# Zeros on TensorE before the queries come, split first loads, half-width value loads and other DMA costs in an order planner

## The chip, the cores and the metric

The kernel runs on one core of one Trainium2 chip, as one launch. The metric is the device time of that launch in microseconds (us), as a median over executions. TensorE (PE) multiplies; VectorE (DVE), ScalarE (ACT) and GpSimd (POOL) work on elements; SyncE (SP) issues nearly all DMAs of this kernel, in order, on one queue.

## What is computed

Three blocks follow one another: attention with a threshold (scores more than tau under their row's maximum get no weight), a token and channel mixer, and a gated two-layer block with a convolution of three taps along the sequence. Four batches (B = 4), 8 heads of 64, 576 rows, 512 channels.

```python
def _attn_ref(q, k, v, tau):                       # q, k, v: (4, 8, 576, 64)
    scores = scale * np.matmul(q, k.transpose(0, 1, 3, 2))
    thresh = np.max(scores, axis=-1, keepdims=True) - tau
    scores = np.where(scores >= thresh, scores, -1000000000.0)
    scores = scores - np.max(scores, axis=-1, keepdims=True)
    attn = np.exp(scores)
    attn = attn / (np.sum(attn, axis=-1, keepdims=True) + 1e-09)
    return np.matmul(attn, v)
...
    h = np.maximum(xt @ w_tok1, 0.0) @ w_tok2      # mixer: over the rows, then over the channels
    u = x + h.transpose(0, 2, 1)
    h2 = np.maximum(u @ w_ch1, 0.0) @ w_ch2
    x = u + h2
...
    h = np.maximum(x @ w_in, 0.0)                  # gated block; conv_w has three taps
    for k in range(K):
        conv_out += conv_w[k][None, None, :] * hp[:, k:k + S, :]
    gate = 1.0 / (1.0 + np.exp(-conv_out))
    return h * gate @ w_out
```

## The kernel before, in words

**Attention.** Per batch there are four pairs of heads, and per pair nine chunks of 128 query rows (`NSL`; the fifth chunk holds the last 64 rows of both heads), so 36 chunks per batch (`PER`). A chunk runs through: `scores` (PE, fp32 in batch 0, L527), the row maximum `nm` (DVE, L548), a threshold (L558), the exponential `e` (ACT, L560), the mask (DVE, L567), an fp16 high part `ph` (ACT, L572) and its low part (POOL, L576), a DMA transpose of both (SP, L581, the tile `pt`), and the product with v (PE, `pv`, L591 and L594). In batch 0 the tiles `e`, `ph` and `pt` of a chunk are pieces of `act_t`, four of each, in turn; later they come from a ring of 15 buffers. `norm`, `tok` and `dense` follow: the token mixer per pair of heads, the channel mixer (L758, L776) and the gated block (L809, L832) per batch. While `dense(b)` runs, `attention(b + 1)` is woven into it. Batch 0's attention has only the conversion of weights beside it.

**Loads.** `prep` loads a pair. q comes in one DMA of 128x576 fp32 (L447) and is scaled by ACT in one instruction (L461); each head's k comes in one of 64x576 (L452). v comes with its rows laid out twice, as nine slots of 64 columns: five slots hold the first layout (rows 0 to 575, 128 at a time), the other four hold the same rows shifted by half a slot. One DMA per head loads all nine (L483, 288 KB). POOL scales them (L492), ACT makes the fp16 high part `vh` of all nine (L493, or L488 for the second head in batch 0), POOL or DVE the low part `vl` of five (L494, L489). Weights come as 64-bit floats in two 32-bit halves (`wload`, L325) and are put together by ACT, DVE and POOL (L362 to L366, L350 to L352). The three taps of the convolution, `conv_w`, are loaded ahead of everything but tau.

**Order.** The instructions are built first; `Order` then puts them on their engines' queues by a list schedule. `cost` has the planned duration of an engine's instruction; `send` has for a DMA the planned time that it takes up the DMA queue, the time to issue it, and its latency; in `run` the DMA queue is one server (`queued`), and a transpose holds SP until the queue is free. Of the instructions that are ready, the one that stands first in the program goes first. The engines then keep that order whatever the chip's times are.

Of the kernel before, what the change touches and what calls it, by code (L numbers as in the profile page):

```python
# [20 lines left out]
class Order:  # L21
# [109 lines left out]
    def send(self, x):  # L131

        i = self.ins[x]
        if i.opcode == "DmaTransposeAnt":
            return 1000, 1300, 1950, 1400
        o, s = self.area(i.outs[0]), self.area(i.ins[0])
        size = o[7] * o[8] * o[6]
        return size / 330 + (50 if size < 1e5 else 0), 500, 1450, 1250 if s[9] and o[9] else 1750 if o[9] else 1300
# [4 lines left out]
    def run(self):  # L143
# [10 lines left out]
        rows, tiled, lands = {}, False, []  # L154
# [20 lines left out]
        for _ in range(n):  # L175
# [4 lines left out]
            if self.dma[x]:  # L180
# [4 lines left out]
                if self.ins[x].opcode == "DmaTransposeAnt":  # L185
                    free[e] = max(free[e], queued)
                if e == "SP":
                    queued = max(queued, t + 700) + work
                    done = max(free[e] + least, queued + land)
                else:  # L190
                    done = max(free[e] + least, t + 700 + work + land)
# [41 lines left out]
def kernel(ctx: ExitStack, tc: tile.TileContext, q, k, v, tau,  # L233
# [7 lines left out]
    nc = tc.nc  # L241
# [38 lines left out]


# [37 lines left out]
    ps = psum.tile([P, 8, 512], F32, name="ps")  # L319
# [85 lines left out]
    if conv_w.dtype == F32:  # L405
        nc.sync.dma_start(cw, conv_w)
    else:
        float32(cw, cw, *load_hl(conv_w, 0, 3 * NG), 0)
# [17 lines left out]
    for vh, _ in v_t:  # L426
        V.memset(vh[:, :, :, D:D + 1], ONE)
    act_t = const.tile([P, NF * 2, S], F16, name="act_t")
# [12 lines left out]
    def prep(b, p):  # L441
# [4 lines left out]
        if b < NB32:  # L446
            nc.sync.dma_start(f32(qt), q[b, p])  # L447
            for h in range(2):
                if b == 0:
# [11 lines left out]
            A.activation(out=t, in_=t, func=AF.Copy, scale=qsc[:, 0:1])  # L461
# [19 lines left out]
        for hh in range(2):  # L481
            t = qk2.tile([P, S], F32, tag="x", name="ld", bufs=15)
            nc.sync.dma_start(t, v[b, 2 * p + hh])  # L483
            vn.append(t.rearrange("p (a d) -> p a d", d=D))
        yield
        for hh in range(2):
            if b == 0 and hh:
                A.activation(out=vh[:, hh, :, 0:D], in_=vn[hh], func=AF.Copy, scale=VSC)  # L488
                V.scalar_tensor_tensor(out=vl[:, hh], in0=vn[hh][:, 0:NS + 1], scalar=VSC, in1=vh[:, hh, 0:NS + 1, 0:D],  # L489
                                       op0=ALU.mult, op1=ALU.subtract)  # L490
            else:
                G.tensor_scalar(out=vn[hh], in0=vn[hh], scalar1=VSC, scalar2=1.0, op0=ALU.mult, op1=ALU.mult)  # L492
                A.activation(out=vh[:, hh, :, 0:D], in_=vn[hh], func=AF.Copy)  # L493
                G.tensor_tensor(out=vl[:, hh], in0=vn[hh][:, 0:NS + 1], in1=vh[:, hh, 0:NS + 1, 0:D], op=ALU.subtract)  # L494
# [370 lines left out]
    for n, _ in enumerate(attention(0)):  # L865
        if n == NW:
# [75 lines left out]
```

## Time and profile before

| | |
|---|---|
| median of 3 executions | 775.82 us |
| lowest and highest | 774.68 and 777.67 us |
| profiled execution | 773.05 us, of which 771.2 us is the span from the first to the last instruction |
| mean granted TensorE clock in the span | 0.993 of full |
| PE busy | 721.5 us, 94% |
| DVE, ACT, POOL busy | 506.5, 459.0, 425.9 us |

The page of the profile has the busy times, a strip of 40 slices of 19.3 us each with the busy tenths of every engine, the granted clock of PE, the DMA load, and the costliest groups of instructions by line. Further views used here: a table of windows (busy time of each engine in a stretch), the timeline (instructions in order of time, neighbours of a kind merged, with the idle time ahead of them and what ended it), the waits (who waited for whom), the groups of instructions by line and shape, and the DMA issues of a stretch with their time from issue to landing.

### The profile page before, as it was taken

Reading aid. Unit: us, or ns where it says so; the run is one execution under the profiler, and the core shown is the slowest. Engines: PE = TensorE matmul, PEld = TensorE weight load, DVE = VectorE, ACT = ScalarE, POOL = GpSimd, SP = SyncE. Lnnn points to the kernel's source line nnn. Section 1 sums busy time; section 2 is a strip of 40 time slices with the busy share of each in tenths; the row PEclk is TensorE's granted clock in tenths of the full one; section 3 lists DMA queues with packets and bytes.
Section 4 is the critical chain, followed back from the end, with each engine's and each line's share of the span. In section 5 each row is a group of like instructions: output and inputs, shape, how many; then the busy total and the mean of one; then the engine's idle time right before and its main releaser. Section 6 shows DMA issues by size and latency. Waiting matters only on the chain. (4 is left out here: it accounts for less than half of the span.)

```text
span 771.2 us, 18502 instructions
## 1 busy us (share of the span) xinstructions
PE 721.5 (94%) x7388; PEld 541.5 (70%) x7388; DVE 506.5 (66%) x913; ACT 459.0 (60%) x926; POOL 425.9 (55%) x463
## 2 busy tenths in 40 slices
PE   5779969999998789999999999999999999999998
PEld 3457757777776646788888766778888766878764
DVE  5968977887779971676867962676876951323470
ACT  6967857786758852576557753675656841211371
POOL 5967778887877990367464850367564830000040
PEclk9999989999999999999999999999999999999999
DMA  9999988999898602568876402577853400000001
GB/s 288 210 217 187 200 193 208 230 230 229 199 238 199 147 27 93 111 153 169 155 142 144 80 23 88 131 136 158 155 123 64 79 29 35 1 1 2 1 1 62
DMA packets 196199, 99.02 MB, mean 128 GB/s; under 512 B 174224, under 2 KB 177808, under 8 KB 196112
## 3 DMA queue, kind: packets, MB, share of 16 engines
q1 hardware_dynamic: 195792, 97.57, 58.2%
q8 instruction: 58, 0.95, 0.5%
q10 hardware_dynamic: 320, 0.26, 0.1%
q14 instruction: 29, 0.24, 0.1%
HBM read 43.54 MB, written 4.72 MB: 63 GB/s over the span
## 5 line engine op out<-in xcount | busy, mean ns | idle before, releaser
L576 POOL TENSOR_TENSOR ph<-e,ph 128x576 f16<-128x576 f32 x108 | 142.5, 1319 | 110.4 <-ACT ph L572 99.3
L776 PE MATMUL ps<-act_t,wc_h 128*128 128x256 f16 (+1 forms) x768 | 149.8, 286 | 0.0
L567 DVE SCALAR_TENSOR_TENSOR e<-ps,thr,e 128x576 f32<-128x576 f32 x108 | 87.9, 814 | 53.6 <-ACT e L560 40.8
L548 DVE TENSOR_REDUCE nm<-ps 128x1 f32<-128x576 f32 x144 | 108.0, 750 | 19.6 <-PE ps L536 10.5
L799 POOL TENSOR_TENSOR act_t<-ct,act_t 128x576 f16<-128x576 f32 x32 | 47.2, 1474 | 128.4 <-ACT act_t L798 127.0
L758 PE MATMUL ps<-u_h,wc_h 128*128 128x320 f16 (+1 forms) x384 | 109.4, 286 | 0.3 <-DVE act_t L733 0.3
L776 PE MATMUL ps<-act_t,wc_l 128*128 128x256 f16 (+1 forms) x384 | 109.7, 286 | 0.0
L758 PE MATMUL ps<-u_h,wc_l 128*128 128x320 f16 (+1 forms) x384 | 109.5, 286 | 0.0
L758 PE MATMUL ps<-u_l,wc_h 128*128 128x320 f16 (+1 forms) x384 | 109.1, 286 | 0.0
L758 PEld LDWEIGHTS <-wc_h 128*128 128x128 f16 x768 | 75.1, 98 | 21.5 <-issue 2.1
L776 PEld LDWEIGHTS <-wc_h 128*128 128x128 f16 x768 | 75.1, 98 | 21.0 <-issue 1.6
L809 PE MATMUL ps<-u_h,wi_h 128*128 128x256 f16 (+1 forms) x256 | 73.2, 286 | 7.1 <-ACT h L785 4.5
L832 PE MATMUL ps<-wo_h,act_t 128*128 128x512 f16 x256 | 76.2, 379 | 0.9 <-POOL act_t L799 0.9
L794 DVE SCALAR_TENSOR_TENSOR ct<-h,cw,ct 128x576 f32<-128x576 f32 x64 | 70.6, 1106 | 8.2 <-ACT ct L792 7.7
L572 ACT ACTIVATE ph<-e 128x576 f16<-128x576 f32 x108 | 73.1, 677 | 1.0 <-DVE e L567 0.8
L733 DVE SCALAR_TENSOR_TENSOR act_t<-ps,act_t 128x256 f16<-128x256 f32 x96 | 43.6, 456 | 45.2 <-ACT act_t L732 44.8
L809 PE MATMUL ps<-u_h,wi_l 128*128 128x256 f16 (+1 forms) x256 | 73.1, 286 | 0.0
L809 PE MATMUL ps<-u_l,wi_h 128*128 128x256 f16 (+1 forms) x256 | 73.1, 286 | 0.0
L591 PE MATMUL ps<-vh,pt 128*128 128x65 f16 (+1 forms) x1080 | 68.3, 194 | 1.0 <-DVE x L614 0.8
L732 ACT ACTIVATE act_t<-ps 128x256 f16<-128x256 f32 x96 | 39.0, 408 | 46.1 <-PE ps L758 45.4
L832 PEld LDWEIGHTS <-act_t 128*128 128x128 f16 x384 | 36.5, 98 | 42.7 <-POOL act_t L799 1.5
L591 PEld LDWEIGHTS <-pt 128*128 128x128 f16 (+1 forms) x1080 | 60.8, 101 | 8.0 <-issue 4.7
(120 smaller groups left out, 1675.0 us busy)
## 6 DMA issues: line engine op xcount, KB each, us to landing
st<-in_moe_w_ch_dram SPq DMA_DIRECT2D x24, 512.0 KB, 4.8
ld<-in_v_dram SPq DMA_DIRECT2D x32, 288.0 KB, 4.1
kt<-ks SPq DMA_DIRECT2D x32, 144.0 KB, 2.8
st<-in_moe_w_in_dram SPq DMA_DIRECT2D x8, 512.0 KB, 4.7
st<-in_moe_w_out_dram SPq DMA_DIRECT2D x8, 512.0 KB, 4.2
out_dram<-ot SPq DMA_DIRECT2D x16, 256.0 KB, 2.0
qt<-in_q_dram SPq DMA_DIRECT2D x8, 288.0 KB, 5.2
kt<-in_k_dram SPq DMA_DIRECT2D x16, 144.0 KB, 4.2
```

The source lines that it names most:

```text
L548: V.tensor_reduce(out=nm, in_=c["s3"], axis=AX.XY, op=ALU.max, negate=True)
L567: V.scalar_tensor_tensor(out=e3, in0=c["s3"], scalar=c["thr"], in1=e3, op0=ALU.is_ge, op1=ALU.mult)
L572: A.activation(out=c["ph"][:, 0:S], in_=c["e"], func=AF.Copy)
L576: G.tensor_tensor(out=c["ph"][:, S:], in0=c["e"], in1=c["ph"][:, 0:S], op=ALU.subtract)
L591: T.matmul(dst[o:o + m], pt[:, j, o:o + m], vh[:, hh, j, 0:D + 1], start=(j == 0), stop=(j == NSL - 1))
L733: V.scalar_tensor_tensor(out=r_t(f, 1)[:, sl], in0=t, scalar=0.0, in1=r_t(f, 0)[:, sl], op0=ALU.max, op1=ALU.subtract)
L758: T.matmul(t, wc1[wx][:, f, c], u[c][ux][:, sl], start=(c == 0 and i == 0), stop=(c == NC - 1 and i == 2))
L776: T.matmul(t, wc2[wx][:, c, f], r_t(f, rx)[:, sl], start=(by_dve(c) and f == 0 and i == 0), stop=(f == NF - 1 and i == 2))
L794: V.scalar_tensor_tensor(out=ct, in0=ht[:, kk:kk + S], scalar=cw[:, kk, f:f + 1], in1=ct, op0=ALU.mult, op1=ALU.add)
L799: G.tensor_tensor(out=g_t(f, 1), in0=ct, in1=g_t(f, 0), op=ALU.subtract)
L809: T.matmul(t, wi[wx][:, f, c], u[c][ux][:, s0:s0 + n], start=(c == 0 and i == 0), stop=(c == NC - 1 and i == 2))
L832: T.matmul(t, g_t(f, gx)[:, j * P:(j + 1) * P], wo[wx][:, f], **lim)
```

## The change

1. PE gets ten matmuls of 128x512 zeros (fp16, from `act_t`, into the PSUM bank that `pv` uses later) as its first work; DVE writes the zeros first of all.
2. The first pair's q is loaded and scaled in two parts, 128 columns and 448 columns, with the first head's k between them.
3. The load of the taps and their conversion moves from the front to step 57 of batch 0's attention (`load_taps`).
4. v is loaded with five slots in place of nine (160 KB in place of 288 KB per head), and POOL and ACT work on five. The other four slots of `vh` are copied inside SBUF by two DMAs per pair, one per half of the partitions, after the high parts are made. Column 65 of `vh` is written too, since the copies read whole rows.
5. The planner's DMA costs change: a transpose takes up the queue for 1100 ns (1000 before), a large copy is planned at 390 bytes per ns and a small one at 300 (330 and 50 ns more for small ones before), and the first copy behind a transpose costs 550 ns more from HBM, 150 ns more from SBUF. All queues are put in order by the new sums.

```diff
         if i.opcode == "DmaTransposeAnt":
-            return 1000, 1300, 1950, 1400
+            return 1100, 1300, 1950, 1400
...
-        return size / 330 + (50 if size < 1e5 else 0), 500, 1450, ...
+        return size / (390 if size > 2e5 else 300), 500, 1450, ...
...
                     free[e] = max(free[e], queued)
+                    turns = True
+                elif turns:
+                    turns, work = False, work + (150 if self.area(self.ins[x].ins[0])[9] else 550)
...
+    V.memset(act_t[:, 0, 0:512], 0.0)
+    for _ in range(10):
+        T.matmul(ps[:, 7], act_t[:, 0, 0:P], act_t[:, 0, 0:512], start=True, stop=True)
...
-            nc.sync.dma_start(f32(qt), q[b, p])
+            first = [slice(0, P), slice(P, S)] if (b, p) == (0, 0) else [slice(0, S)]
+            nc.sync.dma_start(f32(qt)[:, first[0]], q[b, p, :, first[0]])
             for h in range(2):
+                if h and len(first) > 1:
+                    nc.sync.dma_start(f32(qt)[:, first[1]], q[b, p, :, first[1]])
...
-            A.activation(out=t, in_=t, func=AF.Copy, scale=qsc[:, 0:1])
+            for sl in first:
+                A.activation(out=t[:, sl], in_=t[:, sl], func=AF.Copy, scale=qsc[:, 0:1])
...
-            t = qk2.tile([P, S], F32, tag="x", name="ld", bufs=15)
-            nc.sync.dma_start(t, v[b, 2 * p + hh])
+            t = qk2.tile([P, S], F32, tag="x", name="ld", bufs=15)[:, 0:(NS + 1) * D]
+            nc.sync.dma_start(t, v[b, 2 * p + hh, :, 0:(NS + 1) * D])
...
-                A.activation(out=vh[:, hh, :, 0:D], in_=vn[hh], func=AF.Copy)
-                G.tensor_tensor(out=vl[:, hh], in0=vn[hh][:, 0:NS + 1], in1=vh[:, hh, 0:NS + 1, 0:D], op=ALU.subtract)
+                A.activation(out=vh[:, hh, 0:NS + 1, 0:D], in_=vn[hh], func=AF.Copy)
+                G.tensor_tensor(out=vl[:, hh], in0=vn[hh], in1=vh[:, hh, 0:NS + 1, 0:D], op=ALU.subtract)
+            if hh:
+                nc.sync.dma_start(vh[0:D, :, NS + 1:], vh[D:P, :, 0:NS])
+                nc.sync.dma_start(vh[D:P, :, NS + 1:], vh[0:D, :, 1:NS + 1])
...
+        if n == NW // 2:
+            load_taps()
```

Three places show what the new order does on SP's queue. In its rows `st` is a staging tile for weights or taps, `qt` and `kt` are a pair's q and k, `ld` is v as loaded, `vh` its high part, and `act_t<-act_t` is the transpose of a chunk of batch 0. At the start of the program, before:

```order
L296 DMA tau_t<-in_tau_dram 128x1
L325 DMA st<-in_moe_conv_w_dram 128x48
L447 DMA qt_157<-in_q_dram 128x576
L452 DMA kt_0_158<-in_k_dram 64x576
L452 DMA kt_1_159<-in_k_dram 64x576
L483 DMA ld<-in_v_dram 128x576 x2
```

The same place now:

```order
L305 DMA tau_t<-in_tau_dram 128x1
L459 DMA qt_163<-in_q_dram 128x128
L466 DMA kt_0_164<-in_k_dram 64x576
L462 DMA qt_163<-in_q_dram 128x448
L466 DMA kt_1_165<-in_k_dram 64x576
L498 DMA ld<-in_v_dram 128x320 x2
```

The taps are gone from here, a short q comes first, and the rest of q stands behind the first k. From the first weights to the fifth transpose, still on SP, before:

```order
L325 DMA st<-in_moe_w_tok_dram 128x1024 x2
L325 DMA st<-in_moe_w_tok_dram 128x512
L483 DMA ld<-in_v_dram 128x576 x6
L581 DMA_TRANSPOSE act_t<-act_t 128x9x128 x3
L325 DMA st<-in_moe_w_tok_dram 128x576
L581 DMA_TRANSPOSE act_t<-act_t 128x9x128
```

The same place now:

```order
L333 DMA st<-in_moe_w_tok_dram 128x1024 x2
L511 DMA vh_159<-vh_159 64x2x264
L333 DMA st<-in_moe_w_tok_dram 128x512
L498 DMA ld<-in_v_dram 128x320 x5
L599 DMA_TRANSPOSE act_t<-act_t 128x9x128
L512 DMA vh_159<-vh_159 64x2x264
L599 DMA_TRANSPOSE act_t<-act_t 128x9x128 x2
L333 DMA st<-in_moe_w_tok_dram 128x576
L599 DMA_TRANSPOSE act_t<-act_t 128x9x128
```

Five shorter v loads stand where six stood, and the two copies of `vh` came between. In the middle of batch 0's attention, on SP, before:

```order
L325 DMA st<-in_moe_w_ch_dram 128x1024 x2
L581 DMA_TRANSPOSE act_t<-act_t 128x9x128 x3
L325 DMA st<-in_moe_w_ch_dram 128x1024
L447 DMA qt_160<-in_q_dram 128x576
L452 DMA kt_1_162<-in_k_dram 64x576
L581 DMA_TRANSPOSE act_t<-act_t 128x9x128 x6
```

The same place now:

```order
L333 DMA st<-in_moe_w_ch_dram 128x1024 x2
L498 DMA ld<-in_v_dram 128x320
L599 DMA_TRANSPOSE act_t<-act_t 128x9x128 x2
L511 DMA vh_159<-vh_159 64x2x264
L599 DMA_TRANSPOSE act_t<-act_t 128x9x128 x2
L512 DMA vh_159<-vh_159 64x2x264
L599 DMA_TRANSPOSE act_t<-act_t 128x9x128 x2
L459 DMA qt_166<-in_q_dram 128x576
L466 DMA kt_1_168<-in_k_dram 64x576
```

The transposes now stand in shorter groups, with copies of `vh` and one v load between them. From the first to the 36th transpose of batch 0 SP issues 23 other DMAs before and 35 now: nine copies of `vh`, the taps, one v load and one k load more.

## Rows read from the trace of the kernel before

**Rows 1.** The page: span, busy times, and PE's strip of 40 slices.
```profile
span 771.2 us, 18502 instructions
PE 721.5 (94%) x7388; PEld 541.5 (70%) x7388; DVE 506.5 (66%) x913; ACT 459.0 (60%) x926; POOL 425.9 (55%) x463
...
PE   5779969999998789999999999999999999999998
```
**Rows 2.** Windows: stretch, its length, busy us of each engine, clock, DMA share, GB/s.
```profile
0.00:10.00 10.00, 3.68 (x8) 2.71 (x9) 2.98 (x21) 4.04 (x8) 4.37 (x12) 1.00 0.74 201
10.00:20.00 10.00, 6.33 (x26) 3.39 (x24) 8.54 (x17) 9.28 (x16) 6.39 (x6) 1.00 1.07 364
...
120.00:160.00 40.00, 39.66 (x391) 29.73 (x390) 33.64 (x68) 31.18 (x63) 35.59 (x41) 1.00 0.91 224
```
**Rows 3.** Windows again: batch 0's attention, its end, and the weave with batch 1.
```profile
15.00:41.00 26.00, 18.46 (x178) 11.85 (x175) 23.24 (x50) 23.88 (x48) 24.61 (x28) 0.93 1.04 237
41.00:101.00 60.00, 49.90 (x669) 38.24 (x670) 49.75 (x113) 45.69 (x81) 44.35 (x45) 1.00 1.11 201
101.00:114.00 13.00, 8.64 (x91) 6.62 (x92) 7.87 (x17) 6.60 (x12) 9.88 (x12) 0.74 0.87 200
225.00:285.00 60.00, 48.51 (x554) 35.33 (x552) 58.38 (x89) 47.15 (x93) 54.40 (x48) 1.00 0.63 144
```
**Rows 4.** Timeline of the first 24 us: start, length, engine, line, what [idle before, releaser].
```profile
6.32 5.23 PE L527 MATMUL ps<-kt,qt 128*128 128x288 f32 x12 [6.32 <-ACT qt L461]
...
8.62 0.76 DVE L548 TENSOR_REDUCE nm<-ps 128x1 f32<-128x576 f32 x1 [4.25 <-PE ps L527]
...
10.54 0.76 DVE L548 TENSOR_REDUCE nm<-ps 128x1 f32<-128x576 f32 x1 [0.91 <-PE ps L527]
...
12.40 0.81 DVE L567 SCALAR_TENSOR_TENSOR act_t<-ps,thr,act_t 128x576 f32<-128x576 f32 x1
```
**Rows 5.** Groups by line and shape, at 6 to 10.4 us and at 38 to 44 us.
```profile
L527 PE MATMUL ps<-kt,qt 128*128 128x288 f32 x9 | 4.5, 685 | 6.3 <-ACT qt L461 6.3
...
L527 PE MATMUL ps<-kt,qt 128*128 128x288 f32 x12 | 3.6, 428 | 0.0
```
**Rows 6.** DMA issues of short stretches at the start: xcount, KB, us to landing.
```profile
st<-in_moe_conv_w_dram SPq DMA_DIRECT2D x1, 24.0 KB, 2.4
...
qt<-in_q_dram SPq DMA_DIRECT2D x1, 288.0 KB, 3.7
...
kt<-in_k_dram SPq DMA_DIRECT2D x1, 144.0 KB, 3.6
...
act_t<-act_t SPq DMA_TRANSPOSE x1, 5.7
```
**Rows 7.** Timeline of SP's issues.
```profile
1.18 0.42 SPq L325 DMA_DIRECT2D st<-in_moe_conv_w_dram  x1
1.64 0.43 SPq L447 DMA_DIRECT2D qt<-in_q_dram  x1
...
15.32 6.08 SPq L581 DMA_TRANSPOSE act_t<-act_t  x3
...
63.92 1.13 SPq L454 DMA_DIRECT2D kt<-in_q_dram  x2
...
221.56 2.45 SPq L472 DMA_DIRECT2D qt<-qs  x4
```
**Rows 8.** Waits between 15 and 101 us: who waited for whom, us, times, longest.
```profile
PE ps L591 <- DMA act_t<-act_t: 8.5, 7, 2.9
...
ACT act_t L572 <- DMA act_t<-act_t: 6.8, 7, 2.7
PE ps L527 <- DVE act_t L567: 6.8, 6, 2.7
```
**Rows 9.** Groups by line and shape: ACT and POOL at two widths.
```profile
L493 ACT ACTIVATE vh<-ld 128x576 f16<-128x576 f32 x28 | 18.9, 676 | 10.8 <-POOL ld L492 10.8
...
L653 ACT ACTIVATE u_h<-ps 128x320 f16<-128x320 f32 x16 | 6.9, 428 | 3.4 <-PE ps L646 3.2
```

More of the change, by code (lines that the diff above doesn't have):

```diff
@@ L134, in send @@
         if i.opcode == "DmaTransposeAnt":
-            return 1000, 1300, 1950, 1400
+            return 1100, 1300, 1950, 1400
         o, s = self.area(i.outs[0]), self.area(i.ins[0])
         size = o[7] * o[8] * o[6]
-        return size / 330 + (50 if size < 1e5 else 0), 500, 1450, 1250 if s[9] and o[9] else 1750 if o[9] else 1300
+        return size / (390 if size > 2e5 else 300), 500, 1450, 1250 if s[9] and o[9] else 1750 if o[9] else 1300
     LAP = {"DVE": 85, "Activation": 103, "Pool": 44}
@@ L153, in run @@
         end = start = queued = 0.0
-        rows, tiled, lands = {}, False, []
+        rows, tiled, lands, turns = {}, False, [], False
         def offer(x):
@@ L279 @@
     V, A, G, T = nc.vector, nc.scalar, nc.gpsimd, nc.tensor
+    ps = psum.tile([P, 8, 512], F32, name="ps")
+    act_t = const.tile([P, NF * 2, S], F16, name="act_t")
+    V.memset(act_t[:, 0, 0:512], 0.0)
+    for _ in range(10):
+        T.matmul(ps[:, 7], act_t[:, 0, 0:P], act_t[:, 0, 0:512], start=True, stop=True)
     one = const.tile([P, 1], F32, name="one")
@@ L317 @@
     wo = wpair([P, NG, C], "wo")
-    ps = psum.tile([P, 8, 512], F32, name="ps")
     CB = 4
@@ L404, with load_taps @@
     cw = const.tile([P, 3 * NG], F32, name="cw")
[L405 to L408, printed above, removed]
+    taps = cw
+    def load_taps():
+        if conv_w.dtype == F32:
+            nc.sync.dma_start(taps, conv_w)
+        else:
+            float32(taps, taps, *load_hl(conv_w, 0, 3 * NG), 0)
     cw = cw.rearrange("p (k g) -> p k g", k=3)
@@ L426 @@
     for vh, _ in v_t:
-        V.memset(vh[:, :, :, D:D + 1], ONE)
-    act_t = const.tile([P, NF * 2, S], F16, name="act_t")
+        V.memset(vh[:, :, :, D:D + 2], ONE)
     NSL = 2 * NS + 1
@@ L487, in prep @@
             if b == 0 and hh:
-                A.activation(out=vh[:, hh, :, 0:D], in_=vn[hh], func=AF.Copy, scale=VSC)
-                V.scalar_tensor_tensor(out=vl[:, hh], in0=vn[hh][:, 0:NS + 1], scalar=VSC, in1=vh[:, hh, 0:NS + 1, 0:D],
+                A.activation(out=vh[:, hh, 0:NS + 1, 0:D], in_=vn[hh], func=AF.Copy, scale=VSC)
+                V.scalar_tensor_tensor(out=vl[:, hh], in0=vn[hh], scalar=VSC, in1=vh[:, hh, 0:NS + 1, 0:D],
                                        op0=ALU.mult, op1=ALU.subtract)
```

## The prediction

> **What bounds the kernel now.** The page comes first: PE is busy for 721.5 of 771.2 us, and its strip is at 9 from the seventh slice on, with 5 to 9 ahead of that [rows 1]. So PE sets the time for most of the run, and what can be gained is its idle time, 50 us, most of which lies in batch 0's attention. The windows say where: in the first 10 us PE is busy for 3.68 us, in the next ten for 6.33, while from 120 to 160 us it is busy for 39.66 of 40 [rows 2]. From 15 to 101 us it is idle for 26.0 - 18.46 + 60.0 - 49.90 = 17.6 us, and from 225 to 285 us for 11.5 us, where DVE works 58.38 of 60 us [rows 3].
>
> What bounds the start is a chain: q lands, ACT scales it, PE begins at 6.32 us, DVE takes the first maximum at 8.62 and the second at 10.54, the first mask follows at 12.40 [rows 4]. From then on DVE, ACT and POOL are each busy for 89 to 95% of 15 to 41 us [rows 3]. After 41 us none of them is over 83%, and the DMA share is 1.11: here the loop of the transposes counts. A chunk's high part is written over the tile that the transpose four chunks earlier reads, so ACT waits for landings (6.8 us, 7 times), and PE waits for them itself (8.5 us, 7 times); PE's waits for the mask, which frees the PSUM banks, are 6.8 us [rows 8].
>
> **The sum** is made against the profiled execution, 773.05 us: the span of 771.2 and 1.85 around it. The median of the runs is 775.82, 2.8 us more; I take the difference that the sum gives from the median.
>
> **The start (parts 1, 2, 3).** Without the taps the first q load goes out at 1.18 in place of 1.64 us, and the first k at 1.64 [rows 7]. 24 KB landed 2.4 us after issue, 288 KB after 3.7, a k behind 312 KB after 3.6 [rows 6]. The 64 KB of q so land at 3.6 to 4.9, nearer the small load, say 3.9, and k at 4.0 to 5.2, say 4.6. ACT scales 128 columns in under the 0.43 us that 320 take [rows 9]. So data would let PE begin at about 4.6. The zeros stand ahead of it: 10 matmuls of 512 columns are 5120 columns, 2.1 us at 2.4 GHz and 4.3 us at 1.2 GHz (an estimate from the two levels of the clock), from about 1.1 us, when DVE has written them: they end at 3.2 to 5.4. I take the late end, 5.4, 0.9 us ahead of 6.32.
>
> Which level is it? The windows print a clock of 1.00 for the first 10 us, but the same matmul takes 685 ns there and 428 ns at 38 to 44 us [rows 5]: PE began at its lower level. Nine records take 4.5 us there, 0.50 each, and twelve take 3.6 later, 0.30 each. A chunk is four records: 2.0 us cold, 1.2 us warm. If the zeros raise the clock in time, the first maximum can start at 5.4 + 1.2 + 0.3 (the lag in 6.32 + 2.0 to 8.62) = 6.9, 1.7 us earlier; if not, 7.7, 0.9 us earlier. The second chunk needs the rest of q: 432 KB are loaded by then, about what lay up to the first k before (456 KB, landed at 2.1 + 3.6 = 5.7), so 5.3, and 0.6 us of ACT (between the 428 and 676 ns of [rows 9]): 5.9. PE is free at 6.6, ends the chunk at 7.8, and the second maximum comes at 8.1 in place of 10.54, 2.4 us earlier. Since DVE has few gaps from the second maximum on, that is the shift I carry. Its ends: -0.9 (a cold start and no more), and -3.9, which is what the lighter loads would give. Up to the first transpose ten v loads of 288 KB become nine of 160, and the taps go: with one copy of 66 KB more, 1.4 MB less, at the 364 GB/s of 10 to 20 us [rows 2] 3.9 us. That first transpose went out at 15.32 and landed 5.7 us later, behind loads [rows 6, 7]; it will not wait like that again. **-2.4 us**, -0.9 to -3.9.
>
> **ACT and POOL on v (part 4).** 676 ns for 576 columns, 428 for 320 [rows 9]: 0.25 us per head on ACT, and about as much on POOL. Some four of each fall into 15 to 41 us, where both are over 90% busy; later they lie beside PE's work and give nothing. **-0.5 us**, 0 to -1.
>
> **The copies of vh (part 4).** Two per pair, 32 in all, each 66 KB. After batch 0 PE has other work (39.66 of 40 us) and waits for no transpose, so they cost nothing there. In batch 0, between the first transpose and the 36th, SP issues 35 other DMAs in place of 23: nine of these copies and three moved loads. Two k loads took 1.13 us of SP, 0.57 each, and four copies of 72 KB inside SBUF 2.45 us, 0.61 each [rows 7]. In full that is 9 x 0.61 + 3 x 0.57 = 7.2 us on a queue that carries the transposes in order; what stands behind each copy is the next chunk's transpose, and behind that ACT's high part four chunks on. Where the transpose is not what ends last, a copy is free. Of 36 transposes 7 kept PE waiting and 7 kept ACT waiting: a share of 0.19 to 0.39. I take 0.28: **+2.0 us**, 0 to +7.2. `pv` also waits for these copies now; they stand at least a chunk ahead of its own transpose except in the first pair, where the second copy is right behind the first transpose, and that one comes early.
>
> The trace has 72 KB copies landing about as fast as they can be issued, 0.61 us apart [rows 7]. The Trainium skill, "DMA: Bandwidth & Descriptors", section "Rules for kernel authors", speaks against this part: small transfers should be joined into one large, since under 64 KB one pays mostly overhead, and two transfers to the two halves of the partitions should be one. By that rule the copies would be counted in full, and the sum would be -2.4 - 0.5 + 7.2 - 1.4 = +2.9 us in place of -2.3; the row shows that full price and no more, and does not tell what share of it is on the path.
>
> **The order (part 5).** What the planner's numbers do to the queues can't be read from durations. The large loads of 10 to 20 us moved at 364 GB/s [rows 2]: 390 is about as near to it as 330 was, so I see a small improvement at most, in the price of a switch. What an order can change is PE's idle time in the two stretches, 17.6 + 11.5 = 29 us [rows 3]. I credit a twentieth of it, **-1.4 us**, and allow 4 us either way: every later stretch is shuffled too.
>
> **Sum:** -2.4 - 0.5 + 2.0 - 1.4 = -2.3 us: 770.8 for an execution like the profiled one, 775.8 - 2.3 = **773.5 us** for the median. Its own range is 770.5 to 776.5.
>
> **Rivals.**
> *The queue eats the start (slower).* Place: SP and the DMA queue from 41 to 101 us. If the transposes set the pace there throughout, all twelve issues count, 7.2 us, and the start gives 2.4 and v 0.5 back: +4.3, 780.1 us with the order at zero. For it: the share of 1.11 and the 2.03 us per transpose when three go out in a row (6.08 us) [rows 3, 7]. Against it: PE waited for only 7 landings, and as long for masks [rows 8]. It ends slower than the bound of 0.5% (3.9 us) when nearly all of the twelve are on the path, or three quarters of them with an order that loses 1.4 us.
> *The early start is waited away (same).* The loads of the weights and the transposes keep the DMA queue as long as before, the zeros leave the clock low, and only 0.9 us is kept of the start against 0.6 to 1 us of copies: 775.5 us. This is also the case in which the zeros do not do what the change says.
> *The clock does not fall after batch 0's attention (faster).* From 101 to 114 us the mean granted clock is 0.74 [rows 3]: 0.26 x 13 = 3.4 us lost, and behind it PE is never idle, so the loss is on the path. It fell after PE had been idle for much of the time in which the last transposes landed. If the new order fills that gap, 773.5 - 3.4 = 770.1 us; with the lighter loads' full 3.9 us at the start in place of 2.4, 768.6.
>
> **How the numbers follow.** Forecast 0.40 (of it 0.12 below the bound of 0.5%, 771.9 us; 0.28 within), queue 0.19 (0.15 slower, 0.04 within), waited away 0.15 (0.11 within, 0.04 slower), clock 0.26 (all faster). 0.5% is about what a measurement of this kernel can tell from no change. Together faster 0.38, same 0.43, slower 0.19. The range goes from 767.5, a little under the clock's case, to 779.5, a little under the queue's full price.
>
> **What would show it.** Start: PE's first score matmul at about 5.4 us and at 428 ns; second maximum near 8.1; first mask near 10. If the records still take 685 ns, the zeros failed. Early loads: the first transpose lands about 4 us earlier than 21.0 us. Copies: PE's wait for landings between 15 and 101 us about 8.5 us as before if the forecast holds; 12 us or more if the queue eats the start. Clock: the window of the end of batch 0's attention above 0.9 if the third rival holds. POOL and ACT: v's instructions near 430 ns on ACT. What would make the sum wrong is a new wait of `pv` for the copies in batch 0, or a new gap of PE in the woven stretches after 120 us, where I count none.

## The result

The changed kernel takes 778.35 us (median of 12 runs, 775.74 to 781.42), the kernel before 774.33 beside it (12 runs): a ratio of 1.0056, with a 95% interval of 1.0038 to 1.0074. Timed a second time, beside other runs of before, it stood at 1.0074 [1.0049, 1.0099]. The change makes the kernel slower by 0.4 to 1.0%, where I forecast 0.3% faster. The time lies inside the range, but on the side to which I had given 0.19.

The page of after, which answers to [rows 1]:

```profile
span 776.5 us, 18600 instructions
PE 733.1 (94%) x7398; PEld 547.6 (71%) x7398; DVE 508.8 (66%) x914; ACT 452.6 (58%) x927; POOL 418.8 (54%) x463
...
PE   6879789999997789999999999999999999999998
...
PEclk9799889999999989999999999999999999999999
```

The profiled span is 5.3 us longer (776.5 - 771.2). PE is busy for 11.6 us more (733.1 - 721.5) and idle for 6.3 us less (43.4 in place of 49.7). So the change did what it was made for: PE stands idle for less time. Of the 11.6 us the ten matmuls of zeros are 3.92 (row below); the other 7.7 us are the *same* matmuls, taking longer. That is the clock, and the lowest line shows it: it is under 9 in the second, fifth, sixth and one later slice, and the windows give numbers (stretch, length, busy us of PE, PEld, DVE, ACT, POOL, granted clock, DMA share, GB/s). After:

```profile
0.00:10.00 10.00, 7.40 (x23) 3.78 (x24) 4.96 (x25) 5.15 (x9) 4.16 (x12) 1.00 0.69 191
10.00:20.00 10.00, 5.20 (x30) 2.97 (x29) 7.90 (x16) 8.86 (x17) 7.87 (x9) 0.90 1.07 273
15.00:41.00 26.00, 19.89 (x184) 14.28 (x184) 23.77 (x53) 23.08 (x48) 22.35 (x25) 0.80 1.11 221
101.00:114.00 13.00, 9.62 (x111) 6.79 (x109) 9.24 (x21) 7.77 (x15) 10.72 (x13) 0.74 1.05 228
225.00:285.00 60.00, 49.52 (x531) 35.92 (x529) 53.80 (x82) 44.15 (x88) 51.17 (x46) 0.91 0.65 148
```

The clock is 0.80 from 15 to 41 us (0.93 in [rows 3]) and 0.91 from 225 to 285 (1.00 before). A second profile of the same kernel (after_again below) has 0.93, as before, in the first of these stretches, and less of a fall in the other:

```profile
15.00:41.00 26.00, 17.78 (x184) 12.37 (x184) 23.30 (x53) 22.61 (x48) 22.27 (x25) 0.93 1.14 221
225.00:285.00 60.00, 47.53 (x527) 34.18 (x526) 57.58 (x85) 45.06 (x88) 51.94 (x48) 0.97 0.62 143
```

So the fall at 15 to 41 us belongs to one execution, and the one behind 225 us to both. The start, after:

```profile
1.18 3.92 PE L288 MATMUL ps<-act_t 128*128 128x512 f16 x10 [1.18 <-DVE blk L301]
4.94 3.43 PE L545 MATMUL ps<-kt,qt 128*128 128x288 f32 x12
6.11 0.76 DVE L566 TENSOR_REDUCE nm<-ps 128x1 f32<-128x576 f32 x1 [2.38 <-PE ps L545]
8.17 0.75 DVE L566 TENSOR_REDUCE nm<-ps 128x1 f32<-128x576 f32 x1
8.84 0.81 DVE L585 SCALAR_TENSOR_TENSOR act_t<-ps,thr,act_t 128x576 f32<-128x576 f32 x1
```

PE's first score begins at 4.94 (I had 5.4), the second maximum at 8.17 (8.1), the first mask at 8.84 (near 10) in place of 12.40 [rows 4]. The first two are right to 0.5 us, the mask came 1.2 us earlier. The second profile is later: first score at 5.42, its first three records still at 687 ns, second maximum at 9.0, first mask at 9.65. What became of it shows in the starts of later maxima, counted from DVE's records (one per chunk, in us; the first `wc1` matmul of batch 0's dense part beside them):

```
                 2nd    9th   13th   25th   36th   first wc1   last maximum
before          10.5   26.1   35.4   68.7   90.5     115.0        603.5
after            8.2   25.6   35.3   65.7   93.7     116.3        608.7
after, again     9.0   23.9   34.5   65.5   92.8     115.6        606.3
new prices       9.9   25.9   36.0   64.9   86.7     111.0        600.6
```

The 2.3 us of the second maximum are 0.5 at the ninth and 0.1 at the thirteenth; in the second profile 1.5 us become 2.2 and then 0.9, and at the 36th both are behind before. Between the 25th and the 36th after loses 6 us against before. By 115 us 1.3 us are lost in all, and the rest arises between 235 and 300 us: by the number of matmuls begun, after is level with before at 231 us and 5.7 us behind at 280, in its second profile 0.8 ahead and 3.3 behind. Against new_prices 5 us are lost by 115 us already.

### The profile page after: what moved, and what is told of

Read it like the earlier page. It is cut to its first block, busy times and chain, and to the rows that moved or that the text cites. A ratio compares the mean times of both kernels' runs of the same rounds, so it can differ in the third digit from the quotient of the medians.

```text
span 776.5 us, 18600 instructions
## 1 busy us (share of the span) xinstructions
PE 733.1 (94%) x7398; PEld 547.6 (71%) x7398; DVE 508.8 (66%) x914; ACT 452.6 (58%) x927; POOL 418.8 (54%) x463
## 4 chain that ended last, share of the span: by engine, by line
PE 69%; DMA 8%; DVE 7%; POOL 6%; ACT 4%; issue 3%; SPq 2%; POOLq 0%; ACTq 0%; DVEq 0%
PE ps L794 17%; PE ps L776 15%; PE ps L850 10%; PE ps L827 7%; DMA act_t<-act_t 4%; PE ps L554 3%; PE ps L609 3%; PE ps L550 3%; PE ps L649 3%; PE ps L664 2%; DVE ct L812 2%; PE ps L612 2%; POOL ph L594 1%; POOL act_t L594 1%; DVE ct L815 1%
## 5 line engine op out<-in xcount | busy, mean ns | idle before, releaser
L827 PE MATMUL ps<-u_h,wi_h 128*128 128x256 f16 (+1 forms) x256 | 74.9, 293 | 10.9 <-ACT h L803 10.3
L812 DVE SCALAR_TENSOR_TENSOR ct<-h,cw,ct 128x576 f32<-128x576 f32 x64 | 67.2, 1053 | 13.0 <-ACT ct L810 11.8
L827 PE MATMUL ps<-u_h,wi_l 128*128 128x256 f16 (+1 forms) x256 | 74.9, 293 | 0.0
```

The source lines that it names most:

```text
L812: V.scalar_tensor_tensor(out=ct, in0=ht[:, kk:kk + S], scalar=cw[:, kk, f:f + 1], in1=ct, op0=ALU.mult, op1=ALU.add)
L827: T.matmul(t, wi[wx][:, f, c], u[c][ux][:, s0:s0 + n], start=(c == 0 and i == 0), stop=(c == NC - 1 and i == 2))
```

## The experiments

Three theories (A, B and C in the first expectations). The **order theory**: the edits cost little, but the planner makes another, worse order around them. The **queue theory**: the copies and loads cost by themselves, between the transposes. The **clock theory**: what is lost is PE at its lower clock, behind idle stretches. All ratios are to the kernel before, timed beside each; 0.01 is 7.7 us. For a difference of two ratios I give the root of the sum of squares of their half widths.

```
kernel          ratio   95% interval       span    PE busy   PE idle
before          1                          771.2    721.5     49.7
new_prices      0.9966  0.9948 .. 0.9985   768.3    721.3     47.0
price_1150      0.9974  0.9957 .. 0.9991   769.7    725.9     43.8
taps_late       0.9951  0.9929 .. 0.9974   767.5    724.0     43.5
q_frozen        0.9989  0.9965 .. 1.0013   767.2    722.6     44.6
q_parts         1.0023  1.0007 .. 1.0039   773.5    725.8     47.7
v_frozen        1.0001  0.9980 .. 1.0022   767.9    724.5     43.4
v_once          1.0079  1.0050 .. 1.0109   777.2    728.0     49.2
edits_frozen    1.0023  0.9999 .. 1.0046   769.1    726.0     43.1
v_full          1.0032  1.0017 .. 1.0047   769.8    727.5     42.3
no_copies       1.0039  1.0021 .. 1.0057   774.0    731.7     42.3
no_zeros        1.0074  1.0048 .. 1.0101   777.8    727.8     50.0
old_prices      1.0082  1.0058 .. 1.0106   779.4    732.3     47.1
after           1.0056  1.0038 .. 1.0074   776.5    733.1     43.4
after_again     1.0074  1.0049 .. 1.0099   773.9    729.9     44.0
two_moves       1.0055  1.0036 .. 1.0075   773.5    730.0     43.5
fill_after      1.0026  1.0010 .. 1.0042   772.4    738.1     34.3
fill_moves      0.9991  0.9965 .. 1.0016   769.7    739.1     30.6
fill_new        0.9958  0.9933 .. 0.9983   769.7    733.1     36.6
```

Span and PE times are of one profiled run each. The same kernel (after, after_again) differs by 2.6 us between two profiles, and its PE busy time by 3.2: one such span decides nothing under 3 us, and the verdicts go by the ratios.

### The prices alone, and all but the prices

```diff
 old_prices: after, and
-            return 1100, 1300, 1950, 1400
+            return 1000, 1300, 1950, 1400
 ... (and the other two costs as before)
 new_prices: before, with the three new costs and nothing else
```

> The changed kernel with the planner's DMA costs of the kernel before (parts 1 to 4 without part 5). Theory A, the loss is made by the order that the new prices give (PE gaps of 3.8 and 5.4 us at 247 and 266 us, where ACT's queue is blocked): the loss goes, ratio to the kernel before 0.993 to 1.000. Theory B, the copies of vh in the DMA queue make it, whatever the order: ratio 1.004 to 1.008 as for the change, and PE's waits for transposes between 15 and 101 us as long as in the changed kernel. Theory C, the clock: the ratio follows the time at the lower clock, which is 34 us in the changed kernel's trace and 10 us in the one before; 0.5 us of time for each us of it.

> The kernel before with the new DMA costs in its planner and nothing else (part 5 alone). Theory A: slower, ratio 1.004 to 1.010. Theory B: the same as before, 0.997 to 1.003, since no copy is added. Theory C: the time moves by half of what the time at the lower clock does against 10 us.

The new prices alone are *faster* than before, 0.9966. After with the old prices is as slow as after, or slower. So part 5 is not what costs; alone it gives 2.6 us, where I had put 1.4.

### Nine slots of v again; no zeros

```diff
 v_full: after, and
-            nc.sync.dma_start(t, v[b, 2 * p + hh, :, 0:(NS + 1) * D])
+            nc.sync.dma_start(t, v[b, 2 * p + hh])
...
-                nc.sync.dma_start(vh[0:D, :, NS + 1:], vh[D:P, :, 0:NS])
-                nc.sync.dma_start(vh[D:P, :, NS + 1:], vh[0:D, :, 1:NS + 1])
 no_zeros: after, and
-    for _ in range(10):
-        T.matmul(ps[:, 7], act_t[:, 0, 0:P], act_t[:, 0, 0:512], start=True, stop=True)
```

> The changed kernel with v loaded in nine slots again and without the copies inside SBUF (parts 1, 2, 3 and 5). Theory B: the loss goes and the start's gain is left, ratio 0.994 to 0.999. Theory A: the loss stays, 1.003 to 1.008. Theory C: as for the others, half of the change in time at the lower clock.

> The changed kernel without the ten matmuls of zeros and without their memset; every other instruction stands in the same order on its engine. If the zeros give the warm start that the prediction counted on, the second row maximum comes 0.7 to 1.5 us later than in the changed kernel, with the first score matmuls at about 685 ns. If that start is carried to the end, this kernel is 0.7 to 1.5 us slower than the changed one (ratio to the kernel before 1.006 to 1.008). If it is waited away in batch 0's attention, it is within 0.3 us of it.

Without part 4 after loses 0.3% in place of 0.6 to 0.7; against the new prices alone it still loses 0.66% (±0.24). Without the zeros the second maximum is at 8.9 in place of 8.2 us. The zeros do raise the clock: from 4 to 10.4 us a score's record takes 420 ns on the mean in after, 485 in its second profile, 593 without the zeros. The time is that of after, 1.0074 beside 1.0056 and 1.0074: 0.18% (±0.32) or nothing. So no gain of the zeros at the end is shown; the 0.7 to 1.5 us that the expectation would have had are not excluded either.

### Zeros into the idle stretches

```diff
 fill_after: after; fill_new: the kernel of new_prices. Both with
+                    for _ in range(n):   # n for each chosen stretch
+                        T.matmul(ps[:, 7, 328:512], zt[:, 0:P], zt, start=True, stop=True)
```

> The kernel after, its order of work unchanged on every engine, with 187 matmuls of zeros (184 columns each) added in TensorE's order just ahead of the instructions that ended 13 of its 20 idle stretches of at least 0.5 us between 1 and 115 us and between 230 and 292 us; each gets about three quarters of its stretch. They write columns of the eighth PSUM bank that nothing reads. Nothing is taken away, so the output stays the same.
> The clock theory (the time lost is TensorE at the lower granted clock, which follows its idle stretches): of the six spells at the lower clock in the kernel after (34.0 us in all), those at 18.1, 31.7 and 270.7 us have all of the idle time ahead of them covered and vanish (17 us at half speed, 8.5 us of time), those at 86.3 and 106.8 us half of it; so 763 to 772 us, at least 5 us under the kernel after.
> The queue theory (the copies and the later loads delay the data that TensorE waits for) and the order theory (the places of work in the queues are worse): the waits and the order are as they were, and the added work fills time that was idle, so 776 to 780 us.

> The kernel before with the new planner prices alone (the fastest so far, 0.997 of before), its order unchanged, with 167 matmuls of zeros in 11 of its idle stretches in the same way. Its profile has two spells at the lower clock, 3.4 us at 12.9 and 6.8 us at 101.7 us.
> The clock theory: at most 10.2 us at half speed are to be had, 5.1 us, and only the first spell has its idle stretch covered; so 0 to 4 us under the kernel with new prices, 765 to 770 us: a far smaller gain than the same filling gives in the kernel after.
> Queue and order theories: no change, 769 to 771 us.

fill_after took 0.30% (±0.24) off after, 2.3 us, less than half of what the clock theory asked for; against after_again it is 0.48% (±0.30). In the kernel with new prices the same filling gave nothing, 0.08% (±0.31). The starts show where the gain was: at the first `wc1` matmul (115.6 us, against 116.3 and 115.6 in the two profiles of after) there is 0.7 us of it or none, at the first `wo` matmul (276.5 against 280.2 and 277.9) 3.7 or 1.4. Batch 0's attention hardly got faster in this profile, although its clock rose (0.97 from 0 to 120 us, 0.90 and 0.93 in the profiles of after). PE's records say what the clock gave. Without the zeros and the fillers, the 7,388 other matmuls keep PE busy for 719.8 us in fill_after, 729.3 and 725.6 in after, 721.3 in new_prices: nearly all of the lower clock is undone. But the time in which none of them runs is 52.6 us, against 47.1 and 48.3 in after: PE at full clock waits longer. And fill_after is still 0.60% (±0.25), 4.6 us, slower than new_prices. So the lower clock is a part of the loss, and not most of it, unless the fillers cost something themselves; in new_prices they did not.

### Part 4 alone, the split q alone, both planned anew

```diff
 v_once: before with the new prices and part 4
 q_parts: before with the new prices and
+            first = [slice(0, P), slice(P, S)] if (b, p) == (0, 0) else [slice(0, S)]
 ... (both loads and both scalings, as in the change)
```

> The kernel before with the new planner prices and with v loaded once (five slots and the two copies of vh), without the zeros, the split load of q and the later taps.
> The queue theory (the copies in the transposes' queue are what costs): it should lose most of what the kernel after lost against the kernel with new prices (9 us), so 775 to 779 us, 1.004 to 1.009 of before.
> The start theory (zeros, split q, later taps shift the chunks against the transposes, and this costs): close to the kernel with new prices, 769 to 772 us, 0.996 to 1.000.
> The clock theory says which of the two only after the fact: span = 720 us + idle time of TensorE + half of the time at the lower clock, within 2 us, in this kernel too.

> The kernel before with the new planner prices and with q of the first pair loaded and scaled in two parts, nothing else of the change.
> The prediction's step for it: the first scores start up to 2 us earlier, so 766 to 770 us if the gain reaches the end.
> The start theory (an early start costs later): 771 to 776 us, 0.999 to 1.005 of before, with an extra spell at the lower clock within the first 120 us.
> The queue theory: no change from the kernel with new prices, 769 to 771 us.

v alone loses 1.13% (±0.35) against the new prices, 8.7 us; the split q, one load and one scaling more for the same bytes, 0.57% (±0.24). Each is as bad as most of the change. The clock theory's formula, in the expectation for v_once, misses: 720 us, 49.2 idle and half of 20.4 at the lower clock are 779.4 us, for a span of 777.2. In v_once the chunks wait longer for transposes; the waits from 62 to 100 us, first in the kernel with new prices, then in v_once (who waited for whom: us, times, longest):

```profile
ACT act_t L575 <- DMA act_t<-act_t: 1.8, 2, 1.5
...
PE ps L594 <- DMA act_t<-act_t: 0.2, 1, 0.2
```
```profile
ACT act_t L578 <- DMA act_t<-act_t: 5.1, 4, 2.3
...
PE ps L597 <- DMA act_t<-act_t: 2.7, 3, 1.2
```

That could be the copies or the order: the planner moved the work on every queue in dozens of places when the copies came in.

### The same edits with the order held

To tell these apart I took the order that the planner had made for one kernel and gave it to another, as a list for each engine.

```diff
 no_copies: v_full with the order of after
 v_frozen:  v_once with the order of new_prices, the copies put among the transposes as in v_once
 q_frozen:  q_parts with the order of new_prices, the second part behind its neighbour
 price_1150: new_prices, and
-            return 1100, 1300, 1950, 1400
+            return 1150, 1300, 1950, 1400
```

> The kernel after with every engine's order held as the planner gave it there, but v loaded in nine slots as before and the 32 copies of vh gone from SP's queue; nothing else moves.
> The queue theory (what costs is the copies among the transposes themselves, in SP's issuing and in the landings behind them): 4 to 7 us under the kernel after, 771 to 774 us, and the gain has arisen by the end of batch 0's attention (115 us).
> The order theory (what costs is where the planner puts the work once the copies are there): within 1.5 us of the kernel after, 776 to 779 us, with the idle stretch of 5.4 us at 266 us still there.

> The kernel before with the new planner prices, with its order held on every engine, but v loaded once: each of the 32 copies stands in SP's queue behind as many transposes as it does in the kernel with v loaded once that was planned anew (which took 779 us).
> The queue theory: 774 to 778 us, 5 to 8 us over the kernel with new prices.
> The order theory: 769 to 772 us, at most 2 us over it, and no idle stretch over 4 us between 235 and 300 us.

> The kernel before with the new planner prices, with its order held on every engine, and q of the first pair loaded and scaled in two parts (one load more in SP's queue, behind the first load of k, and one scaling more on ACT).
> The order theory (the 4.4 us that the same edit lost when it was planned anew come from other places of work, since the order moved from the third chunk on): 767 to 771 us, like the kernel with new prices or up to 2 us under it.
> The start theory (an early start costs later, whatever the order): 772 to 775 us.

> The kernel before with the new planner prices, but 1150 ns in place of 1100 ns for a transpose's time on the queue: no work is added or taken away, only the planned order moves by about as much as it does for the split load of q. A control: how far a mere reordering moves the time.
> The order theory: anything from 766 to 778 us; over 2 us from the kernel with new prices (769.5 us) says that such reordering is worth as much as the edits.
> The queue and start theories: within 2 us of it, 768 to 771.5 us.

With the order held, v once costs 0.35% (±0.28), 2.7 us, where planned anew it costs 1.13: the new order is worth 0.78% (±0.36), 6.0 us. The split q costs 0.23% (±0.30), nothing that can be told from zero, against 0.57: 0.34% (±0.29) is order. And after's order stays bad with the copies gone: 1.0039, 0.17% (±0.25) under after and 0.35% (±0.31) under after_again. The control moved about as many places as the split q did, for no edit, and stayed at 0.08% (±0.25): not every reordering costs.

### All edits but the taps at the good order; two moves in the bad one

In after's order the longest idle stretch of PE stands at 266 us. PE, then ACT and DVE (start, length, line, and in brackets the idle time before it and who ended it):

```profile
264.12 0.27 PE L827 MATMUL ps<-u_h,wi_l 128*128 128x256 f16 x1
264.23 0.27 PE L827 MATMUL ps<-u_l,wi_h 128*128 128x256 f16 x1
...
271.76 0.37 PE L827 MATMUL ps<-u_h,wi_h 128*128 128x256 f16 x1 [5.40 <-ACT h L803]
271.93 0.42 PE L827 MATMUL ps<-u_h,wi_l 128*128 128x256 f16 x1
272.14 0.42 PE L827 MATMUL ps<-u_l,wi_h 128*128 128x256 f16 x1
```
```profile
270.75 0.68 ACT L816 ACTIVATE act_t<-ct 128x576 f16<-128x576 f32 x1 [3.03 <-DVE ct L815]
271.34 0.37 ACT L803 ACTIVATE h<-ps 128x256 f32<-128x256 f32 x1
```
```profile
264.85 3.63 DVE L812 SCALAR_TENSOR_TENSOR ct<-h,cw,ct 128x576 f32<-128x576 f32 x2
268.41 0.68 DVE L372 SCALAR_TENSOR_TENSOR ps<-st,ps 128x512 int32<-128x512 int32 x1
269.00 1.72 DVE L815 SCALAR_TENSOR_TENSOR ct<-ct,h 128x576 f32<-128x576 f32 x1
```

PE waits for a bank that ACT empties at 271.34 (L803). That stands in ACT's queue behind L816, which waits for DVE's L815, and that stands behind two L812, the second of which belongs to the next gate. Before the stretch the 256-column matmuls start 0.11 us apart (2.4 GHz), behind it 0.21 (1.2 GHz). Every order planned with the copies has this stretch (4.6 to 5.7 us, no_copies too, which has none to wait for); in those of new_prices, q_parts and v_full there are in its place four or five of 1.3 to 1.9 us, and the clock stays at 1.00 from 235 to 300 us.

```diff
 edits_frozen: before, new prices, zeros, split q, v once; the order of new_prices (taps as before)
 two_moves: after, its order held but for
-ACT:  vh, wo_h, ct, act_t, vh, h      DVE:  ct (next gate), ps, ct (L815)
+ACT:  h, vh, wo_h, ct, act_t, vh      DVE:  ps, ct (L815), ct (next gate)
```

> All edits of the change together but the later taps (new planner prices, zeros, q of the first pair in two parts, v loaded once with the 32 copies), with every engine's order held at the one that the planner gave the kernel before under the new prices; the copies stand in SP's queue behind as many transposes as in the kernel with v loaded once.
> The order theory (the edits themselves cost little, the order that the planner makes around them costs 5 us or more): 768 to 774 us, 0.996 to 1.003 of before, and no idle stretch over 4 us between 235 and 300 us.
> The queue theory (the copies and the early start cost directly): 775 us or more, 1.004 and up, like the kernel after.

> The kernel after with its order held, but for two instructions: on ACT the eviction of h that stood behind a scaling of v (the wait of 2.29 us at 245 us) goes ahead of it, and on DVE the multiply that ends a gate (at 269.0 us) goes ahead of the first multiply of the next gate. Nothing is added or taken away.
> The order theory with the clock theory: the idle stretch of 3.76 us at 246.8 us falls under 1.5 us, that of 5.40 us at 266.4 us to about 3.5 us, one or both spells at the lower clock behind them (3.4 and 6.8 us) go, and the time falls by 3 to 8 us, to 770 to 775 us.
> The queue theory: these places have nothing to do with the copies or the start, so at most the 1 us by which TensorE waits less, 776 to 778 us.

All edits but the later taps at the good order: 1.0023, 0.33% (±0.30) under after, but still 0.57% (±0.30) over the new prices alone. So of what after loses against new_prices (0.90%, 6.9 us) some 4.4 us are the edits themselves and 2.5 the order with the taps; I had expected it on the order's side more clearly. This kernel also prices the early start: against v_frozen, at the same order, it has the zeros and the split q more, and its second maximum comes at 7.8 in place of 10.3 us; yet its first `wc1` matmul comes at 115.3 in place of 113.8, and its ratio is 0.22% (±0.32) higher, 1.7 us (±2.4). In the profile of two_moves the idle stretch of 5.40 us (5.67 in after_again) is 3.44. The other one, 3.76 us at 247 us, is 2.23, but in after_again, with nothing moved, there are two of 1.62 and 1.50 in its place, and the clock from 235 to 300 us is 0.97 in both. The timed runs show no gain, 0.01% (±0.27): unclear by itself.

### After again, and both together

```diff
 after_again: after, unchanged
 fill_moves: two_moves, with zeros in twelve of its idle stretches
 taps_late: the kernel of new_prices, and
+        if n == NW // 2:
+            load_taps()
```

> The kernel after once more, unchanged, so that it stands on the same chip and beside the same runs of before as the two kernels that follow.
> Every theory: 1.004 to 1.0075 of before, lower-clock time of 24 to 34 us in its profile.

> The kernel after with its order held but for the two moves (the eviction of h ahead of a scaling of v on ACT, the last multiply of a gate ahead of the next gate's first on DVE), and with 184 matmuls of zeros in twelve of the idle stretches that are left, as in the kernel after with fillers.
> The clock theory with the order theory: less idle ahead of the spells and less of the lower clock than either alone (under 10 us in the profile), so 1.000 to 1.003 of before, 2 to 5 us under the kernel after on the same chip.
> The queue theory: as the kernel after, 1.004 to 1.007.

> The kernel before with the new planner prices and the later taps, nothing else of the change: the last of its five parts that has not been run by itself.
> The prediction's step for it (the queue is one load shorter ahead of q): 767 to 770 us, 0 to 2 us under the kernel with new prices.
> The order theory: the order moves little (under 1 in 100 places), so 768 to 772 us.
> The start theory (an early start costs later): 771 to 774 us.

fill_moves is at 0.9991, 0.83% (±0.36) under after on the same chip: 6.4 us, all that the change had lost against before. Its page, then that of after_again:

```profile
span 769.7 us, 18972 instructions
PE 739.1 (96%) x7582; PEld 557.1 (72%) x7582; DVE 509.1 (66%) x915; ACT 453.0 (59%) x927; POOL 419.1 (54%) x463
```
```profile
span 773.9 us, 18600 instructions
PE 729.9 (94%) x7398; PEld 545.1 (70%) x7398; DVE 510.6 (66%) x914; ACT 453.3 (59%) x927; POOL 419.6 (54%) x463
```

The window behind batch 0's attention in both, fill_moves first (its clock is 1.00):

```profile
120.00:300.00 180.00, 170.16 (x1753) 123.50 (x1751) 140.06 (x251) 122.34 (x238) 141.85 (x144) 1.00 0.76 180
```
```profile
120.00:300.00 180.00, 166.56 (x1706) 120.29 (x1704) 144.02 (x254) 123.43 (x241) 142.29 (x145) 0.99 0.79 179
```

And what stands in fill_moves where the stretch of 5.40 us was, on PE's timeline:

```profile
262.56 2.70 PE L395 MATMUL ps<-zt 128*128 128x184 f16 x32
266.18 0.27 PE L938 MATMUL ps<-u_h,wi_h 128*128 128x256 f16 x1 [0.92 <-ACT h L914]
```

The sum of the two profiles, over the records of the 7,388 other matmuls as above: they keep PE busy for 720.7 us in fill_moves, 725.6 in after_again, 721.5 before. PE does nothing useful for 769.7 - 720.7 = 49.0 us, in after_again for 48.3. So nothing was won on waits; the 4.2 us between the two spans are 4.9 us of matmuls that run faster, less 0.7 us of waits. That is the clock theory's own mark, and the control fits: in new_prices the matmuls take 721.3 us, as in before, and 720.6 with 167 fillers. There is little to win, and the 0.7 us are less than the 2.1 that the waits grow by.

The two moves show beside fill_after, which has nearly the same clock: fill_moves is 0.35% (±0.30), 2.7 us, faster, and its PE waits for 49.0 us in place of 52.6. The fillers of the two are not quite the same, so this price is a rough one.

taps_late is the best by its median (768.29 us, 0.9951); against new_prices its 0.15% (±0.29) can't be told from nothing. Both beat the kernel before and after.

## Why the prediction was wrong

**The start (-2.4): the times right, the step "that is the shift I carry" wrong.** In the first profile the first score, its record at 423 ns, the second maximum and the first mask came as written or earlier; in the second they came up to 0.9 us later than written, but for the mask. I held that DVE's few gaps would carry the shift to the end. They did not: where I had -2.4 us, the zeros and the split q at the good order show +1.7 (±2.4, edits_frozen against v_frozen), and in the table of maxima the shift is all but gone by the thirteenth. q_frozen alone, 0.23% (±0.30) slower, says less: its second maximum is 0.5 us earlier than in new_prices, but at the held order its first mask is not (12.3 against 11.8). Why the shift is lost is argued, not shown: a chunk also needs its transpose, and that one lands when the queue comes to it. The first transpose of each kernel (DMA issues at 15.2 us, or 15.1 for the second: line, count, us to landing), new_prices, then q_parts, then after:

```profile
act_t<-act_t SPq DMA_TRANSPOSE x1, 6.2
```
```profile
act_t<-act_t SPq DMA_TRANSPOSE x1, 6.1
```
```profile
act_t<-act_t SPq DMA_TRANSPOSE x1, 4.2
```

With the split q it goes out at 15.43 against 15.29 and lands 6.1 us later, so no earlier than without. In after, with lighter loads ahead of it, it lands at 15.26 + 4.2 = 19.5 us, 1.5 earlier than before (18.8 in the second profile); I had written "about 4 us earlier" and "it will not wait like that again". The rival *The early start is waited away* names this, though by another way (the clock did rise).

**The copies (+2.0, 0 to 7.2): right as far as the runs can tell.** v_frozen puts all of part 4 at +2.7 us (±2.2), where copies and shorter v work together made +1.5 in my sum; no_copies, at the other order, takes 1.3 (±1.9) off after and 2.7 (±2.4) off after_again. No wait of `pv` for a copy stands among the waits. PE's waits for landings from 15 to 101 us were 7.5 us, where 12 would have meant the queue's rival. v on ACT takes 459 ns (I had near 430).

```profile
ACT act_t L590 <- DMA act_t<-act_t: 9.0, 8, 2.6
PE ps L545 <- DVE act_t L585: 8.3, 7, 2.4
PE ps L609 <- DMA act_t<-act_t: 7.5, 7, 2.4
```

Against [rows 8] ACT's wait rose by 2.2, PE's for masks by 1.5, PE's for landings fell by 1.0. The Trainium skill's rule on small transfers ("DMA: Bandwidth & Descriptors", "Rules for kernel authors"), by which I had worked out +2.9 in all, comes nearer to the result than my sum; but the held order shows the copies at 2.7 us, not at the full 7.2, so it is near for another reason.

**The order (-1.4 ± 4): the prices right, the independence wrong.** Alone they give 2.6 us. My sum took the order as one term beside the others. But the planner makes the whole order anew for each edit, and what it made around the copies costs 6.0 us more than the same copies at the order it had (v_once against v_frozen), around the split q 2.6. In the whole change it is 2.5 us (±2.3). The last sign that I had given of a wrong sum, a new gap of PE in the woven stretches where I counted none, is what came: 5.40 us at 266 us.

**The clock: no term of the sum.** I let it enter as a gain only (the third rival, one spell at 101 to 114 us; the clock there stayed at 0.74). I counted idle time of PE, and that fell as hoped, by 6.3 us, 2.4 more than the zeros fill. I did not ask whether the idle time that is left lies in longer pieces. From 235 us on it did, and over the whole span the same matmuls, by their records, took 7.8 us longer in one profile, 4.1 in the other. So "The sum" fails here too: its terms are waits, and the same matmuls were taken to cost the same.

In sum, against before: prices -2.6 us, the edits +4.4, the order around them, with the taps, +2.5 (each ±2.3 or less), which by the way they are taken add up to the 0.56%. My sum had -2.4 - 0.5 + 2.0 = -0.9 for the edits and -1.4 for prices and order, which measured -0.1 together. So of the 6.6 us by which it missed, 5.3 are the edits, most of it the start's gain that never arrived, and 1.3 the order. The clock is no further term beside these: it is one way in which they reach the end. Fillers alone undo it and win 2.3 us (3.7 against after_again); fillers and two moves win 6.4, with every edit still in place. Open: what makes the zeros and the split q cost time at a held order, how much of the edits' own 4.4 us runs over the clock, since edits_frozen was not run with fillers, and what the moves are worth, which showed nothing alone.

## What to carry to other kernels

Where an engine is busy for 94% of the time, do not sum only its idle time: ask also what its work will cost behind each idle stretch, and compare its busy time for the same instructions before and after. An edit given to a planner is two edits; hold the old order and run the new code in it, and the two can be priced apart. An early start is worth only what the next queue on the path lets through.

## What the runs showed of the hardware

- The same 256-column matmuls start 0.11 us apart ahead of a PE idle stretch of 5.40 us and 0.21 us behind it. 32 matmuls of zeros in such a stretch (3.44 us long in two_moves) kept them at 0.11 in fill_moves: zeros were work enough to hold PE's clock up there.
- Two executions of one program differ in where the clock falls: PE's busy time was 733.1 us in one profile of after, 729.9 in another, and the spans differ by 2.6 us.
- DVE's multiply-add of 128x576 (L812) took 0.80 us at 271.24 and 1.8 us (3.63 for two) at 264.85. Through the slow two POOL was at subtractions (1.30 us from 264.82, 1.81 from 266.06); at 271.24 POOL had been idle since 270.1, and its next subtraction began at 271.51, behind the start of L812. So it is with all 64 in the trace of after: the 18 with no work of POOL beside them took 0.80 to 0.82 us, and so did the 11 beside which POOL's subtraction began 0.09 us or more behind their start; in each of the 25 that took over 1 us, a subtraction was running when L812 started, or began within 0.03 us. The slow two stand in the chain ahead of the stretch at 266 us. I had not looked for this, and no run here changes it by itself. The Trainium skill ("GPSIMD Engine Reference", section "1. Specifications") says that POOL shares its SBUF interfaces with DVE, with contention for DVE instructions that read two SBUF operands, as L812 does; the rows agree where POOL was first, and show no contention where L812 was.
